# Fourteen of 24 attention units turn their keys by VectorE blocks and transfers through DRAM instead of TensorE transposes

## The chip, the cores and the metric

The kernel runs on one core of one Trainium2 chip. The metric is the device time of one execution in microseconds (us); lower is better. Times are medians of several executions; the profile is of one further execution. In it PE is TensorE's matmuls and PEld its weight loads, DVE is VectorE, ACT ScalarE, POOL GpSimd and SP SyncE, which here only issues transfers (DMAs).

## The reference: what is computed

A gated linear attention over 4 batches, 8 heads, 768 steps and head size 48, whose output goes, as 3072 tokens of 384 features, through a gated two-layer network of width 1536, all in float32:

```python
for t in range(S):
    state = alpha[:, :, t, :, None] * state + np.einsum('bhd,bhe->bhde', k[:, :, t], v[:, :, t])
    y[:, :, t] = np.einsum('bhd,bhde->bhe', q[:, :, t], state)
x = y.transpose(0, 2, 1, 3).reshape(B * S, H * D)
gate = 1.0 / (1.0 + np.exp(-(x @ w_gate)))
out = (gate * (x @ w_val)) @ w_out
```

## The kernel before

**Tiles and stages.** The tokens go in six groups of 512. For each group the attention has four units, one for every two heads, so 24 units, and the network has twelve steps (f = 0 to 11), one for every 128 of the 1536 hidden features, so 72 steps. Features lie on partitions and tokens along the rows of a tile. The first units run before the network starts; from unit 8 on one unit is woven into every third network step, for the group after the one that the network is at.

**A step** (`step`, L692 on; its products in `products`, L237) multiplies x with the gate and value weights into two of three PSUM banks `gv`, nine matmuls each (three feature tiles, times three because x and the weights are split into a high and a low part). ACT takes the sigmoid of the gate (sg, L705), DVE multiplies (L707), ACT rounds the product to its high part hh (L708), DVE takes the rest hl (L709), and PE adds their products with the output weights into three banks `po` (L717), hh with six matmuls and hl with three, a step or more later.

**A late unit** (`late`, from L590 on) works on chunks of 64 tokens, its two heads on partitions 0 to 47 and 64 to 111. SP loads the first decays of each chunk, the decays and the keys into a tile `in` (L594; two of them). DVE scans the decays from the back into G (L407) and from the front into F (L411), with a few small operations between (L409, L410, L413: the chunk factors dec); POOL multiplies the keys by G in place (L415); ACT copies the chunk starts of G away (L417). SP loads the queries into A (L604), the values v (L606) and their second layout vs (L609); DVE multiplies A by F (L612). The keys have to stand once as they are, for the scores, and once with tokens on partitions (kn), for the states: `turn` transposes them on PE, four matmuls with the identity into a `gv` bank (L428), and ACT copies the bank to kn (L432). There is one kn tile after the first units. Then PE makes the scores (L625) and the states' additions (adds, L631), DVE masks the scores (L641) and runs the states (L654), POOL scales them (L661), and a period later PE makes the outputs (L673). `finish` copies them out (L439), moves them through DMAs to their place in x (L446), where ACT and DVE split x into its two parts (L453, L455).

**What sets the order.** `Plan` collects every operation with a cost, a due time and its readers and writers, plays them through by its own costs and writes each engine's instructions in that order; no engine chooses at run time. A unit's due times are set in `begin` by network steps: y is the step at which the unit is visited, x the one of the unit before, three steps earlier. A transfer counts there by its bytes alone, at 390 GB/s and a fixed share. `SHIFTS` moves the due times of numbered operations.

Of the kernel before, what the change touches and what calls it, by code (L numbers as in the profile page):

```python
# [8 lines left out]
F32 = mybir.dt.float32  # L9
# [9 lines left out]
P = 128  # L19
B, H, S, D = 4, 8, 768, 48  # L20
DM, DF = 384, 1536
C = 128
R = 64
E = 64
# [5 lines left out]
T = 512  # L30
# [7 lines left out]
CH, EH = T // C, T // E  # L38
# [8 lines left out]
def after(key, more):  # L47
    return None if key is None else key + more
# [138 lines left out]
RATE = 390e3  # L187
# [7 lines left out]
def vec(n):  # L195
    return 0.07 + n / 960
# [44 lines left out]
def chunked(ctx, tc, rows, vc, vh, vg, weights_in, out, const, ident, flags, weights, within):  # L241
    nc = tc.nc
    sb = ctx.enter_context(tc.tile_pool(name="sb", bufs=1))
    ps = ctx.enter_context(tc.tile_pool(name="ps", bufs=1, space=bass.MemoryType.PSUM))
    plan = Plan()
# [46 lines left out]
    for tag in ("w11", "w8"):  # L292
        nm, t = borrow(tag, WF + 2)
# [6 lines left out]
    r_kn = ring("kn", 1, CH, P, early=[borrow("w6", CH, P) for _ in range(2)])  # L300
# [10 lines left out]
    starts = sb.tile([P, NG * NP, EH], F32, name="starts")  # L311
# [4 lines left out]
    r_hh, r_hl = ring("hh", 2, T, dtype=F32R), ring("hl", 2, T, dtype=F32R)  # L316
    r_at, r_gv, r_po = ring("at", 2, 512, pool=ps), ring("gv", 3, 512, pool=ps), ring("po", NM, 512, pool=ps)
    r_bank = Ring([r_gv.tiles[1], *r_at.tiles, r_gv.tiles[2]])
    ob = [(f"raw{i // 2}", raws[i // 2][1].bitcast(F32)[:, i % 2 * T:(i % 2 + 1) * T]) for i in range(NM)]

    nc.vector.memset(d1g[C], 0.0)
# [78 lines left out]
    def decays(u, size, t, inn, tin):  # L400

        n, nch = T, T // size
        a0, az, kT = tin[:, 0:nch], tin[:, A_Z:A_K], tin[:, A_K:A_Q]
        over = ["later"] if size == E else []
        (gn, G), (fn, F), (g0n, G0), (decn, dec) = r_G.next(), r_F.next(), r_G0.next(), r_dec.next()
        G0, dec = G0[:, 0:nch], dec[:, 0:nch]
        plan.add("vector", scan(n), t["G"], lambda: nc.vector.tensor_tensor_scan(  # L407
            out=G[:, ::-1], data0=az[:, n:0:-1], data1=d1g[size], initial=0.0, op0=ALU.mult, op1=ALU.add), [(inn, "a"), *over], [gn], port=True)
        plan.add("vector", 0.08, t["G"], lambda: nc.vector.tensor_tensor(out=G0, in0=G[:, 0:n:size], in1=tiny[:, 0:nch], op=ALU.max), [gn], [g0n], port=True)  # L409
        plan.add("vector", 0.09, t["G"], lambda: nc.vector.reciprocal(out=d1f[:, 0:n:size], in_=G0), [g0n], ["d1f"])  # L410
        plan.add("vector", scan(n), after(t["G"], 0.01), lambda: nc.vector.tensor_tensor_scan(  # L411
            out=F, data0=az[:, 0:n], data1=d1f, initial=0.0, op0=ALU.mult, op1=ALU.add), ["d1f", (inn, "a")], [fn], port=True)
        plan.add("vector", 0.07, t["dec"], lambda: nc.vector.tensor_tensor(out=dec, in0=a0, in1=G[:, 0:n:size], op=ALU.mult), [gn, (inn, "a")], [decn], port=True)  # L413
        e = "vector" if u in KEYS else "gpsimd"
        plan.add(e, vec(n) if u in KEYS else pool_(n), t["kt"], lambda: getattr(nc, e).tensor_tensor(  # L415
            out=kT, in0=kT, in1=G, op=ALU.mult), [gn, (inn, "r")], [(inn, "k")], port=True)
        plan.add("scalar", 0.14, t["flag"], lambda: nc.scalar.copy(out=starts[:, u, 0:nch], in_=G[:, 0:n:size]), [gn], [("start", u)])  # L417
        return fn, F, decn, dec

    def bound(u, t, fn, F):  # L420
        plan.add("scalar", act(T) + 0.13, t["flag"], lambda: nc.scalar.activation(  # L421
# [2 lines left out]
    def turn(t, inn, kT, pkn, pk):  # L424

        def turned():
            for c in range(CH):
                nc.tensor.transpose(out=pk[:, c * P:(c + 1) * P], in_=kT[:, c * P:(c + 1) * P], identity=ident)  # L428

        plan.add("tensor", (0.109 * CH + 0.03, 0.9), t["X"], turned, [(inn, "k")], [pkn])  # L430
        knn, kn = r_kn.next()
        plan.add("scalar", act(CH * P), t["kn"], lambda: nc.scalar.copy(  # L432
            out=kn.rearrange("p c d -> p (c d)"), in_=pk[:, 0:CH * P]), [pkn], [knn])
        return knn, kn

    def finish(g, p, t, pyn, py):
# [23 lines left out]
    def unit(u, g, p, t):  # L460

        n, nch = T, CH
        inn, tin = r_in.next()
        for lo, hi, marks in ((0, A_K, "a"), (A_K, WIDTH, "rkq")) if u < NP else ((0, WIDTH, "arkq"),):
            plan.add("sync", (0.475, P * (hi - lo) * 4 / RATE), t["load"] if u else -3000.0 + lo, lambda lo=lo, hi=hi: nc.sync.dma_start(
                out=tin[:, lo:hi], in_=rows[g, p, :, lo:hi]), writes=[(inn, m) for m in marks])
        if g:
            vn, v = r_v.next()
            plan.add("sync", (0.475, P * CH * 2 * D * 4 / RATE), after(t["load"], 0.2), lambda: nc.sync.dma_start(
                out=v.rearrange("p c j e -> p (c j e)"), in_=vc[g, p]), writes=[(vn, "v")])  # L470
        else:
            vn, vw = r_vg.next()
            plan.add("sync", (0.475, P * CH * GAP * 4 / RATE), t["load"] if u else -1500.0, lambda: nc.sync.dma_start(
                out=vw.rearrange("p c e -> p (c e)"), in_=vg[p]), writes=[(vn, "v")])
            v = vw.rearrange("p c (o e) -> p c o e", o=1)
            v = [vw[:, :, R * j:R * j + D] for j in range(2)]
        vj = (lambda c, j: v[:, c, j]) if g else (lambda c, j: v[j][:, c])
        kT, qT = tin[:, A_K:A_Q], tin[:, A_Q:WIDTH]
        fn, F, decn, dec = decays(u, C, t, inn, tin)
        e = t["e_q"]  # L480
        plan.add(e, vec(n) if e == "vector" else pool_(n), t["q"], lambda: getattr(nc, e).tensor_tensor(
            out=qT, in0=qT, in1=F, op=ALU.mult), [(inn, "r"), fn], [(inn, "q")], port=True)
# [21 lines left out]
        an, A = r_A.next()  # L504
# [85 lines left out]
    def late(u, g, p, t):  # L590
# [3 lines left out]
        plan.add("sync", (0.475, P * A_Q * 4 / RATE), t["load"], lambda: nc.sync.dma_start(  # L594
            out=tin[:, 0:A_Q], in_=rows[g, p, :, 0:A_Q]), writes=[(inn, m) for m in "ark"])
        kT = tin[:, A_K:A_Q]
        fn, F, decn, dec = decays(u, E, t, inn, tin)
        pkn, pk = r_gv.next()
        knn, kn = turn(t, inn, kT, pkn, pk)
        (an, A), (vn, v), (vsn, vs) = r_A.next(), r_v.next(), r_vs.next()  # L600
        own = [slice(R * j, R * j + R) for j in range(2)]
        other = own[::-1]
# [32 lines left out]
            scores()  # L635
            adds()

        plan.add("tensor", (0.13 * EH + 0.1, 0.5), t["A"], both, [(inn, "k"), (an, 2), (an, 3), knn, (vn, "v")], [x[0] for x in pas])
        for j, (pan, pa) in enumerate(pas):
            for i in range(2):  # L640
                plan.add("vector", 0.43, t["mask"], lambda pa=pa, j=j, i=i: nc.vector.tensor_tensor(  # L641
# [111 lines left out]
    def visit(u):  # L753

        return NF * (u // NP - 1) + 7 - 3 * (NP - 1 - u % NP)

    def begin(u):
        g, p = divmod(u, NP)
        if u < EARLY:
            t = dict.fromkeys(("load", "G", "dec", "kt", "q", "X", "kn", "Y", "A", "mask", "S", "sd", "out", "y"))  # L760
            t.update(flag=14.0 + u, run=1, e_q="vector" if u in QUERIES else "gpsimd")
            return unit(u, g, p, t)
        if u < 2 * NP:
            t = dict.fromkeys(("load", "more", "G", "dec", "kt", "q", "kn", "X", "A", "mask", "S", "sd", "out", "y"))
            return late(u, g, p, {**t, "flag": 14.0 + u})
        y, x = visit(u), visit(u - 1)
        t = dict.fromkeys(("load", "more", "G", "dec", "kt", "q", "kn"))
        if True:
            t = dict(load=x - 2.5, G=x - 0.9, kt=x - 0.7, dec=x, kn=x + 0.6, more=y - 2.0, q=y - 1.0)
        t.update(flag=y + 1 + 0.5 * p, X=after(x, 0.53), A=y + 0.5, mask=y + 0.6, S=y + 0.65, sd=y + 1.2, out=visit(u + 1) + 0.52, y=None)  # L770
        return late(u, g, p, t)

    n_units = NG * NP
# [48 lines left out]
CASTS = ((3, 0), (4, 0), (5, 0), (8, 0), (9, 1))  # L822
QUERIES = (0, 1, 4)
KEYS = (0, 1, 3, 4, 6, 7)
SHIFTS = ((5, -2), (12, -4), (51, 8), (52, 5), (54, 8), (71, 6), (82, 2), (85, 1), (93, -8), (126, 3), (143, 4), (160, 9), (170, 1), (177, 5), (179, 2), (187, 10), (219, -1), (222, 21), (237, -1), (282, 12), (290, -5), (302, 3), (324, 3), (325, -4), (338, 4), (343, -8), (347, -13), (348, -1), (355, 2), (360, 2), (370, 2), (373, 6), (374, 9), (376, 6), (388, 2), (402, 2), (403, 4), (416, -4), (418, 6), (440, -5), (464, -10), (468, 34), (480, -3), (493, 5), (494, 4), (503, -2), (519, 16), (565, -3), (573, -2), (583, 6), (588, -2), (598, -1), (601, 7), (622, -4), (658, 3), (695, 2), (795, 12), (817, 8), (848, 2), (851, -1))
WARM = 29
APART = 24


# [162 lines left out]
```

## Time and profile before

| | |
|---|---|
| median of three runs | 522.94 us (522.88 to 524.06) |
| the profiled execution | 524.13 us, of which the span from its first to its last instruction is 522.4 us |
| PE, PEld, DVE, ACT, POOL busy | 511.0, 434.4, 335.8, 181.9, 95.8 us |
| granted TensorE clock, mean | 0.996 |

The page puts the engine of the last-ending chain beside the busy shares. Busy time is of one engine over the whole span; what a stretch of the program waits for is read from its windows and its timeline. A timeline row merges equal instructions that follow each other: start, length, engine, line, operation, output <- inputs, count, and in brackets the engine's idle time before it and what ended it.

### The profile page before, as it was taken

The page shows a single profiled execution, that of the slowest core. Times are in us where ns is not written, and L with a number is a line of the kernel's source. Part 1 is how long each engine was busy: PE and PEld are TensorE (multiplying, and loading weights), DVE is VectorE, ACT ScalarE, POOL GpSimd, SP SyncE. Part 2 cuts the span into 40 slices and gives each one's busy share as a digit, 9 for nine tenths or more (in the row PEclk, how much of TensorE's full clock was granted, in tenths as well). Part 3 has the DMA queues.
Part 4 walks back from the last instruction along what each step waited for, and adds up shares of the span by engine and source line. Part 5 has one row for each costly group of instructions (what it writes and reads, how often), then busy time and mean ns, then how long its engine had stood idle before and what let it go on. Part 6 is the DMA issues. An engine that isn't in the chain of part 4 may idle for free.

```text
span 522.4 us, 10493 instructions
## 1 busy us (share of the span) xinstructions
PE 511.0 (98%) x4279; PEld 434.4 (83%) x4279; DVE 335.8 (64%) x646; ACT 181.9 (35%) x343; POOL 95.8 (18%) x112
## 2 busy tenths in 40 slices
PE   8999999999999999999999999999999999999994
PEld 4878888788888888888888888888888888888884
DVE  7899999998856884657558648567666342222222
ACT  2447665663323233223233323232323222211221
POOL 4450202213303320302213123032021010000000
PEclk9999999999999999999999999999999999999998
DMA  8747985661321311502303503213312000100001
GB/s 317 285 139 229 310 267 180 186 198 60 107 80 29 107 60 48 168 14 93 107 2 107 163 6 108 81 28 107 120 48 53 1 15 16 61 0 0 2 1 65
DMA packets 22647, 51.83 MB, mean 99 GB/s; under 512 B 3520, under 2 KB 8896, under 8 KB 22592
## 3 DMA queue, kind: packets, MB, share of 16 engines
q1 hardware_dynamic: 22160, 50.22, 30.5%
q0 software_dynamic: 432, 0.88, 1.0%
q8 instruction: 34, 0.56, 0.4%
q14 instruction: 21, 0.17, 0.1%
HBM read 41.55 MB, written 4.72 MB: 89 GB/s over the span
## 4 chain that ended last, share of the span: by engine, by line
PE 85%; DVE 11%; DMA 1%; issue 1%; ACT 0%; DVEq 0%
PE gv L237 49%; PE po L717 26%; PE gv L673 3%; PE at L625 2%; PE gv L428 2%; DMA in<-in_rows_dram 1%; DVE G L407 1%; DVE F L411 1%; DVE w L379 1%; PE at L631 1%; DVE raw L369 1%; DVE first_w L369 1%; DVE hl L709 1%; DVE gv L707 0%; PE at L493 0%
## 5 line engine op out<-in xcount | busy, mean ns | idle before, releaser
L237 PE MATMUL gv<-x,w 128*128 128x512 f32 x1296 | 302.5, 380 | 1.1 <-DVE st L521 0.7
L237 PEld LDWEIGHTS gv<-x,w 128*128 128x128 f32 x1296 | 244.0, 189 | 37.5 <-DVE st L521 1.1
L707 DVE TENSOR_TENSOR gv<-gv,sg 128x512 f32<-128x512 f32 x72 | 50.2, 697 | 140.0 <-PE gv L237 138.5
L717 PE MATMUL po<-hh,w 128*128 128x512 f32 x432 | 109.6, 385 | 0.1
L717 PEld LDWEIGHTS po<-hh,w 128*128 128x128 f32 x432 | 79.7, 189 | 12.3 <-ACT hh L708 0.7
L661 POOL TENSOR_TENSOR vs<-st,dec 64x384 f32<-64x384 f32 x36 | 41.8, 1160 | 260.8 <-DVE st L654 259.5
L708 ACT CAST hh<-gv 128x512 fp32r<-128x512 f32 x72 | 42.1, 585 | 130.1 <-DVE gv L707 124.2
L705 ACT ACTIVATE sg<-gv 128x512 f32<-128x512 f32 x72 | 42.9, 596 | 108.4 <-PE gv L237 106.9
L709 DVE TENSOR_TENSOR hl<-gv,hh 128x512 fp32r<-128x512 f32 x72 | 49.5, 687 | 20.9 <-ACT hh L708 18.8
L717 PE MATMUL po<-hl,w 128*128 128x512 f32 x216 | 60.7, 381 | 0.0
L717 PEld LDWEIGHTS po<-hl,w 128*128 128x128 f32 x216 | 40.7, 189 | 6.5 <-DVE hl L709 0.9
L654 DVE SCALAR_TENSOR_TENSOR st<-st,dec,at 128x48 f32<-128x48 f32 x144 | 38.0, 264 | 4.3
L407 DVE TENSOR_TENSOR_SCAN G<-in,d1g 128x512 f32<-128x512 f32 x22 | 33.8, 1534 | 3.7 <-DMA in<-in_rows_dram 1.8
L641 DVE TENSOR_TENSOR A<-at,mask 64x256 f32<-64x256 f32 x72 | 30.2, 419 | 3.7 <-PE at L631 3.0
L612 DVE TENSOR_TENSOR A<-A,F 64x512 f32<-64x512 f32 x36 | 28.6, 795 | 0.9 <-DMA A<-in_rows_dram 0.3
L415 POOL TENSOR_TENSOR in<-in,G 128x512 f32<-128x512 f32 x17 | 23.0, 1350 | 26.3 <-PE gv L428 17.3
L411 DVE TENSOR_TENSOR_SCAN F<-in,d1f 128x512 f32<-128x512 f32 x22 | 26.8, 1220 | 0.5
L421 ACT ACTIVATE F<-F 128x512 f32<-128x512 f32 x23 | 14.5, 630 | 18.8 <-DVE A L612 16.3
L673 PEld LDWEIGHTS gv<-A,vs 128*48 128x48 f32 x576 | 17.1, 123 | 3.4 <-DVE A L641 2.2
L673 PE MATMUL gv<-A,vs 128*48 128x64 f32 x576 | 19.8, 222 | 0.0
L625 PEld LDWEIGHTS at<-A,in 48*64 48x64 f32 x576 | 10.2, 134 | 6.7 <-issue 5.6
L428 PE MATMUL gv<-ident,in 128*128 128x128 f32 x88 | 14.2, 285 | 0.8 <-DVE in L415 0.6
(136 smaller groups left out, 335.7 us busy)
## 6 DMA issues: line engine op xcount, KB each, us to landing
in<-in_rows_dram SPq DMA_DIRECT2D x18, 516.5 KB, 4.4
raw<-in_w_dram SPq DMA_DIRECT2D x14, 577.0 KB, 4.0
first_w<-in_w_dram SPq DMA_DIRECT2D x8, 577.0 KB, 4.6
A<-in_rows_dram SPq DMA_DIRECT2D x36, 128.0 KB, 3.7
out_dram<-raw SPq DMA_DIRECT2D x18, 256.0 KB, 2.2
v<-in_vc_dram SPq DMA_DIRECT2D x20, 192.0 KB, 4.8
vs<-in_vh_dram SPq DMA_DIRECT2D x36, 96.0 KB, 3.4
x<-yt SPq DMA_DIRECT2D x30, 96.0 KB, 2.8
```

Of the source, the lines that this page charges most:

```text
L237: nc.tensor.matmul(out=dst, lhsT=lhs(a, i), rhs=rhs(b, i), start=(n == 0 and i == 0), stop=(n == len(todo) - 1 and i == NK - 1))
L407: plan.add("vector", scan(n), t["G"], lambda: nc.vector.tensor_tensor_scan(out=G[:, ::-1], data0=az[:, n:0:-1], data1=d1g[size], initial=0 ...
L411: plan.add("vector", scan(n), after(t["G"], 0.01), lambda: nc.vector.tensor_tensor_scan(out=F, data0=az[:, 0:n], data1=d1f, initial=0.0, o ...
L641: plan.add("vector", 0.43, t["mask"], lambda pa=pa, j=j, i=i: nc.vector.tensor_tensor(out=A[other[j], j].rearrange("p (c i t) -> p i c t", ...
L654: nc.vector.scalar_tensor_tensor(out=st[:, c + 1, :], in0=st[:, c, :], scalar=dec[:, c:c + 1], in1=pas[c % 2][1][:, T // 2 + c // 2 * D:T ...
L661: plan.add("gpsimd", pool_(EH * D), t["sd"], lambda j=j: nc.gpsimd.tensor_tensor(out=vs[own[j], j], in0=st[own[j], 0:EH], in1=dec[own[j]]. ...
L673: nc.tensor.matmul(out=py[R * j:R * j + D, cs], lhsT=vs[r, j, c, :], rhs=A[r, j, cs], start=True, stop=True)
L705: plan.add("scalar", act(T), first(0.3), lambda: nc.scalar.activation(out=sg, in_=got["g"][1][:, 0:T], func=AF.Sigmoid), [got["g"][0]], [sgn])
L707: plan.add("vector", vec(T), first(0.4), lambda: nc.vector.tensor_tensor(out=pv, in0=pv, in1=sg, op=ALU.mult), [sgn], [pvn])
L708: plan.add("scalar", act(T), first(0.45), lambda: nc.scalar.copy(out=hh, in_=pv), [pvn], [hhn])
L709: plan.add("vector", vec(T), first(0.5), lambda: nc.vector.tensor_tensor(out=hl, in0=pv, in1=hh, op=ALU.subtract), [pvn, hhn], [hln])
L717: nc.tensor.matmul(out=pso_now[m][1][:, 0:T], lhsT=weights.part("o", b, f)[:, m * P:(m + 1) * P], rhs=halves(h[a]), start=(f == 0 and i == ...
```

## The change

From unit 10 on (`CARRIED = 10`; 14 units) PE's transposes and ACT's copy go. In `carry`, DVE transposes the decayed keys in blocks of 32x32 into G, whose values nobody needs any longer then; SP stores the blocks to a DRAM tile `way` and loads them back into kn in four transfers, one for each 32 partitions, so that each block comes to its place. A block's rows are 32 numbers, so every contiguous piece of these transfers is 128 bytes. ACT's copy of the chunk starts of G gets its own due time, ahead of the transpose. The matmuls of a unit's scores and adds wait for all four loads. The numbers in `SHIFTS` are moved with the added operations; nothing else of the table differs.

```diff
+    dram = ctx.enter_context(tc.tile_pool(name="dram", bufs=1, space=bass.MemoryType.DRAM))
+    r_way = Ring([(f"way{i}", dram.tile([16, P, 32], F32, name=f"way{i}")) for i in range(2)])
...
-        plan.add("scalar", 0.14, t["flag"], lambda: nc.scalar.copy(out=starts[:, u, 0:nch], in_=G[:, 0:n:size]), [gn], [("start", u)])
-        return fn, F, decn, dec
+        plan.add("scalar", 0.14, t.get("first", t["flag"]), lambda: nc.scalar.copy(out=starts[:, u, 0:nch], in_=G[:, 0:n:size]), [gn], [("start", u)])
+        return fn, F, decn, dec, gn, G
...
+    def carry(t, inn, kT, gn, G):
+
+        plan.add("vector", vec(T), t["turn"], lambda: nc.vector.transpose(
+            out=G.rearrange("p (m c j) -> p m c j", m=4, c=CH), in_=kT.rearrange("p (c m i) -> p m c i", c=CH, m=4)), [(inn, "k")], [gn], port=True)
+        wn, way = r_way.next()
+        plan.add("sync", (0.475, P * T * 4 / RATE), t["away"], lambda: nc.sync.dma_start(
+            out=way.rearrange("x (b i) j -> (b i) x j", b=4), in_=G.rearrange("p (x j) -> p x j", j=32)), [gn], [wn])
+        knn, kn = r_kn.next()
+        for m in range(4):
+            plan.add("sync", (0.475, P * C * 4 / RATE), t["back"], lambda m=m: nc.sync.dma_start(
+                out=kn[32 * m:32 * m + 32].rearrange("p c (b j) -> p (c b) j", b=4),
+                in_=way[CH * m:CH * m + CH].rearrange("c (b i) j -> i (c b) j", b=4)), [wn], [(knn, m)])
+        return knn, kn
...
-        fn, F, decn, dec = decays(u, E, t, inn, tin)
-        pkn, pk = r_gv.next()
-        knn, kn = turn(t, inn, kT, pkn, pk)
+        fn, F, decn, dec, gn, G = decays(u, E, t, inn, tin)
+        carried = "turn" in t
+        if carried:
+            knn, kn = carry(t, inn, kT, gn, G)
+        else:
+            pkn, pk = r_gv.next()
+            knn, kn = turn(t, inn, kT, pkn, pk)
...
-        plan.add("tensor", (0.13 * EH + 0.1, 0.5), t["A"], both, [(inn, "k"), (an, 2), (an, 3), knn, (vn, "v")], [x[0] for x in pas])
+        plan.add("tensor", (0.13 * EH + 0.1, 0.5), t["A"], both, [(inn, "k"), (an, 2), (an, 3), knn, *((knn, m) for m in range(4)), (vn, "v")], [x[0] for x in pas])
...
+        if u >= CARRIED:
+            t.update(first=x - 0.6, turn=x - 0.4, away=x - 0.2, back=x + 0.6)
...
+CARRIED = 10
```

**What moves.** On PE at a unit's visit, before: `at` and `gv` are PSUM banks, `kn` the turned keys, `in` the input tile with the decayed keys, `ident` the identity.

```order
L631 MATMUL at_120<-v_80,kn_85 48x48 x2
L428 MATMUL gv_122<-ident,in_79 128x128 x4
L673 MATMUL gv_121<-A_88,vs_90 48x64 x16
L717 MATMUL po_124<-hh_116,w_1050 128x512 x2
L717 MATMUL po_125<-hh_116,w_1050 128x512 x2
L717 MATMUL po_126<-hh_116,w_1050 128x512 x2
L237 MATMUL gv_123<-x_681,w_1287 128x512 x9
```

The same place now (line numbers are 20 higher or so):

```order
L651 MATMUL at_120<-v_80,kn_85 48x48 x2
L693 MATMUL gv_122<-A_88,vs_90 48x64 x16
L737 MATMUL po_124<-hh_116,w_1054 128x512 x2
L737 MATMUL po_125<-hh_116,w_1054 128x512 x2
L737 MATMUL po_126<-hh_116,w_1054 128x512 x2
L237 MATMUL gv_123<-x_685,w_1291 128x512 x9
```

The transposes are gone from between the adds and the outputs; nothing else moved at this place.

On SP, one unit of a group's middle, before: `in` is the input load, `x<-yt` the outputs' way to x.

```order
L594 DMA in_78<-in_rows_dram 128x1033
L606 DMA v_80<-in_vc_dram 128x384
L604 DMA A_88<-in_rows_dram 64x512 x2
L609 DMA vs_90<-in_vh_dram 64x384 x2
L446 DMA x_681<-yt_86 32x512
L446 DMA x_681<-yt_86 16x512
L446 DMA x_681<-yt_86 48x512
```

And now:

```order
L443 DMA way_130<-G_92 128x16x32
L610 DMA in_78<-in_rows_dram 128x1033
L447 DMA kn_85<-way_130 32x16x32 x4
L624 DMA A_88<-in_rows_dram 64x512 x2
L629 DMA vs_90<-in_vh_dram 64x384 x2
L626 DMA v_80<-in_vc_dram 128x384
L462 DMA x_685<-yt_86 32x512
L462 DMA x_685<-yt_86 16x512
L462 DMA x_685<-yt_86 48x512
```

The store stands ahead of the next input load, the four loads of kn between it and A, and v has gone behind vs; x keeps its place at the end.

On PE at the end of a group, before: `x_112` with `w_395` is the first product of the new group, `po` the output banks of the old one.

```order
L717 MATMUL po_124<-hl_117,w_1165 128x512
L237 MATMUL gv_122<-x_112,w_395 128x512 x9
L717 MATMUL po_125<-hl_117,w_1165 128x512
L717 MATMUL po_126<-hl_117,w_1165 128x512
L237 MATMUL gv_123<-x_112,w_395 128x512 x9
L717 MATMUL po_125<-hh_116,w_1287 128x512 x2
```

And now:

```order
L737 MATMUL po_124<-hl_117,w_1169 128x512
L737 MATMUL po_125<-hl_117,w_1169 128x512
L737 MATMUL po_126<-hl_117,w_1169 128x512
L737 MATMUL po_125<-hh_116,w_1291 128x512 x2
L737 MATMUL po_124<-hh_116,w_1291 128x512 x2
L737 MATMUL po_126<-hh_116,w_1291 128x512 x2
L237 MATMUL gv_122<-x_112,w_399 128x512 x9
L237 MATMUL gv_123<-x_112,w_399 128x512 x9
```

The new group's first products have gone behind two hl and six hh matmuls of the old one; so at two of the group ends. DVE's transpose stands in most units right behind dec (L413, now L415), or behind the subtraction of x (L455, now L471) where one stands there, and ahead of the next gate product.

## Rows read from the trace of the kernel before

**Rows 1.** The page: busy us by engine, one queue, the last-ending chain.

```profile
PE 511.0 (98%) x4279; PEld 434.4 (83%) x4279; DVE 335.8 (64%) x646; ACT 181.9 (35%) x343; POOL 95.8 (18%) x112
...
q1 hardware_dynamic: 22160, 50.22, 30.5%
...
PE 85%; DVE 11%; DMA 1%; issue 1%; ACT 0%; DVEq 0%
```

**Rows 2.** Windows: stretch, length, busy PE, PEld, DVE, ACT, POOL, clock, DMA share, GB/s.

```profile
320.00:360.00 40.00, 40.00 (x361) 34.59 (x361) 25.59 (x53) 12.45 (x24) 8.24 (x8) 1.00 0.24 70
```

**Rows 3.** Timeline of PE over one period: start us, length us.

```profile
313.44 0.69 PE L625 MATMUL at<-A,in 48*64 48x64 f32 x32
...
314.43 0.66 PE L428 MATMUL gv<-ident,in 128*128 128x128 f32 x4
315.01 1.10 PE L673 MATMUL gv<-A,vs 128*48 128x64 f32 x32
...
329.10 2.11 PE L237 MATMUL gv<-x,w 128*128 128x512 f32 x9
...
333.72 0.70 PE L625 MATMUL at<-A,in 48*64 48x64 f32 x32
```

**Rows 4.** Line 428 from 120 to 400 us: count, ns min/median/max, first, last start.

```profile
L428 PE MATMUL gv<-ident,in x56: 272/273/332, 131.8 to 395.9; 128*128 128x128 f32 x56
```

**Rows 5.** Groups by form on DVE: count, busy us, mean ns, idle before.

```profile
L407 DVE TENSOR_TENSOR_SCAN G<-in,d1g 128x512 f32<-128x512 f32 x22 | 33.8, 1534 | 3.7 <-DMA in<-in_rows_dram 1.8 <-POOL vs L661 1.7 <-issue 0.2
...
L737 DVE COPY raw<-po 128x512 f32<-128x512 f32 x5 | 3.4, 681 | 0.0
```

**Rows 6.** Timeline of POOL, the keys times G.

```profile
321.70 1.28 POOL L415 TENSOR_TENSOR in<-in,G 128x512 f32<-128x512 f32 x1
```

**Rows 7.** Timeline of DVE in the same period.

```profile
322.86 1.39 DVE L612 TENSOR_TENSOR A<-A,F 64x512 f32<-64x512 f32 x2
324.28 0.69 DVE L709 TENSOR_TENSOR hl<-gv,hh 128x512 fp32r<-128x512 f32 x1
...
326.46 0.15 DVE L413 TENSOR_TENSOR dec<-in,G 128x8 f32<-128x8 f32 x1
326.53 0.69 DVE L455 TENSOR_TENSOR x<-x 128x512 fp32r<-128x512 f32 x1
328.07 0.70 DVE L707 TENSOR_TENSOR gv<-gv,sg 128x512 f32<-128x512 f32 x1 [0.86 <-PE gv L237]
```

**Rows 8.** DMA from 289.5 to 293.9: rate in 40 slices, queue (packets, MB, share), issue to landing.

```profile
GB/s 0 0 0 0 0 0 0 0 0 0 242 428 354 335 465 354 354 335 447 372 354 428 391 335 372 428 354 372 354 75 0 0 0 0 0 149 0 0 0 0
...
q1 hardware_dynamic: 432, 0.79, 47.9%
...
out_dram<-raw SPq DMA_DIRECT2D x3, 256.0 KB, 2.3
```

**Rows 9.** DMA from 313 to 326, a unit's transfers: queue and one load.

```profile
q1 hardware_dynamic: 752, 1.38, 36.1%
...
in<-in_rows_dram SPq DMA_DIRECT2D x1, 516.5 KB, 3.4
```

**Rows 10.** Waits of SP's queue: total us, times, longest.

```profile
SPq L594 <- PE at L625: 128.4, 14, 14.7
```

**Rows 11.** Timeline of SP, the input load.

```profile
314.23 0.33 SPq L594 DMA_DIRECT2D in<-in_rows_dram  x1
```

**Rows 12.** Timeline of PE and DVE at the end of a group.

```profile
362.54 1.46 PE L717 MATMUL po<-hh,w 128*128 128x512 f32 x6
362.81 0.70 DVE L707 TENSOR_TENSOR gv<-gv,sg 128x512 f32<-128x512 f32 x1 [1.24 <-PE gv L237]
363.42 0.68 DVE L455 TENSOR_TENSOR x<-x 128x512 fp32r<-128x512 f32 x1
...
363.84 0.38 PE L717 MATMUL po<-hl,w 128*128 128x512 f32 x1
...
364.05 2.11 PE L237 MATMUL gv<-x,w 128*128 128x512 f32 x9
```

More of the change, by code (lines that the diff above doesn't have):

```diff
@@ L478, in unit @@
         kT, qT = tin[:, A_K:A_Q], tin[:, A_Q:WIDTH]
-        fn, F, decn, dec = decays(u, C, t, inn, tin)
+        fn, F, decn, dec, gn, G = decays(u, C, t, inn, tin)
         e = t["e_q"]
@@ L824 @@
 KEYS = (0, 1, 3, 4, 6, 7)
-SHIFTS = ((5, -2), (12, -4), (51, 8), (52, 5), (54, 8), (71, 6), (82, 2), (85, 1), (93, -8), (126, 3), (143, 4), (160, 9), (170, 1), (177, 5), (179, 2), (187, 10), (219, -1), (222, 21), (237, -1), (282, 12), (290, -5), (302, 3), (324, 3), (325, -4), (338, 4), (343, -8), (347, -13), (348, -1), (355, 2), (360, 2), (370, 2), (373, 6), (374, 9), (376, 6), (388, 2), (402, 2), (403, 4), (416, -4), (418, 6), (440, -5), (464, -10), (468, 34), (480, -3), (493, 5), (494, 4), (503, -2), (519, 16), (565, -3), (573, -2), (583, 6), (588, -2), (598, -1), (601, 7), (622, -4), (658, 3), (695, 2), (795, 12), (817, 8), (848, 2), (851, -1))
+SHIFTS = ((5, -2), (12, -4), (51, 8), (52, 5), (54, 8), (71, 6), (82, 2), (85, 1), (93, -8), (126, 3), (143, 4), (160, 9), (170, 1), (177, 5), (179, 2), (187, 10), (219, -1), (222, 21), (237, -1), (282, 12), (290, -5), (302, 3), (324, 3), (325, -4), (338, 4), (343, -8), (347, -13), (348, -1), (355, 2), (360, 2), (370, 2), (373, 6), (374, 9), (376, 6), (388, 2), (402, 2), (403, 4), (416, -4), (418, 6), (440, -5), (464, -10), (468, 34), (480, -3), (493, 5), (494, 4), (503, -2), (519, 16), (565, -3), (573, -2), (583, 6), (588, -2), (598, -1), (601, 7), (622, -4), (658, 3), (699, 2), (803, 12), (829, 8), (860, 2), (863, -1))
 WARM = 29
+CARRIED = 10
 APART = 24
```

## The prediction, before the change was run

> **What bounds the kernel now.** I read the busy shares first: TensorE (PE) is busy 511.0 of 522.4 us, VectorE (DVE) 335.8, ScalarE 181.9, GpSimd 95.8, and the chain that ended last is 85% PE [rows 1]. A busy PE may still hide waits, so I read the stage that the change touches by its windows: from 320 to 360 us PE is busy 40.00 of 40.00 us at full granted clock, while the DMA engines are used to 0.24 and DVE 25.6 of 40 us [rows 2]. So in this stretch a microsecond taken from PE's list is a microsecond of the run, unless something else comes late. The timeline of PE then gives the period: the score matmuls of two successive units start at 313.44 and 333.72, 20.28 us apart [rows 3]. The change asks two questions: what do the transposes occupy on PE, and does the new way of kn, through 4096 small pieces a unit, fit into 20 us.
>
> **What goes.** The four transposes of a unit start at 314.43 and the output matmuls behind them at 315.01: 0.58 us of PE's list, not the 0.66 us of modelled busy time [rows 3]. From 120 us on there are 56 of them, so 14 units of four [rows 4]: 14 x 0.58 = 8.1 us. The output matmuls need the masks and states of the unit before, a period old, so they can move up at once. ScalarE's copy of kn also goes; ScalarE waits most of its time, so it counts nothing.
>
> **What DVE gets.** One transpose of 128x512 per unit, which the trace does not show. The nearest rows of that shape are a copy at 681 ns and, as upper end, a scan at 1534 ns [rows 5]; I take 0.69 us. It needs the decayed keys, which GpSimd has at 322.98 [rows 6], and stands behind dec, at 326.6, or behind the x subtraction, at 327.2. The next DVE instruction waits for PE until 328.07 [rows 7], so 0.69 us fits, and 1.53 us would delay the gate product by 0.7 us. The PE step that eats such a product comes microseconds later: hl, ended by 324.97, holds a bank that PE takes at 329.10 [rows 3, 7]. That is 4.1 us of slack, and hides either end. The starts copy, now due before the turn writes over G, is a 0.2 us item of an engine with room, and G's next writer comes a period later, when the store has long read it.
>
> **The waits that come in.** The turn waits for the keys, and behind it stands the gate product; the store waits for the turn, and behind it the next input load, which waits for PE in any case; the kn loads wait for the store's landing and for the adds that free kn, and behind them stand A, vs, v and the x transfers; the adds wait for kn, and behind them the outputs. As built, a transfer also waits for the landing of the eighth before it; with 14 a unit in place of 9 the x transfers so wait for kn, which is ahead of them in the queue anyway.
>
> **What the queue gets.** Per unit one store of 2048 pieces of 128 B and four loads of 512 such pieces, 128 pieces for each of the 16 DMA engines both ways. Call their data times w and k. No row shows pieces of this size. A dense store of three times 128 rows of 2 KB kept the engines busy for 47.9% of 4.4 us, 33.7 us summed over 16, for 432 packets; its best slice ran at 465 GB/s, 29 bytes per ns and engine, so 0.79 MB are 27.2 us and 6.5 us are left, 15 ns per packet [rows 8]. A 128 B piece is then 15 + 4 = 19 ns, and w = 128 x 19 ns = 2.5 us. The same sum for a unit's loads (36.1% of 13 us x 16 = 75.1 us, 47.6 of them bytes, 752 packets) leaves 37 ns per packet, 41 ns for a piece and 5.3 us [rows 9]. The lower end is bytes alone, 0.6 us; the upper end is that a piece costs what a 2 KB packet does, 33.7 / 384 = 88 ns, 11.2 us. The new transfers are long and dense like the store, the loads' engines were often between transfers, so I take w = 2.5 and k = 3.2, with 5.3 as k's likely top.
>
> Does it fit? The wait for the store's landing costs nothing while it ends before SP turns to the loads. The store is issued when the turn ends, about 328.0 - 20.3 = 307.7 for the loads at 314.7; it lands after 1.6 us (2.3 less 0.7 of data [rows 8]) plus w, 311.8. SP had been idle there: it waits 128.4 us in 14 times for the input buffer that the scores free [rows 10]. The kn loads then stand right behind the input load (issue 314.23, landing 3.4 us later, 317.6 [rows 9, 11]) and in front of A and vs, which wait behind them. A lands at 317.6 + k + 0.7 for its own bytes: 321.5 at k = 3.2, 323.6 at 5.3. Its first reader is DVE's A multiply at 322.86, 322.3 in the shorter period [rows 7]. So A is in time, or 1.3 us late, inside the 4.1 us. kn itself is needed a period later.
>
> There is a loop in it, and it gives the limit: A lands, A multiply to dec 3.75 us, x 0.69, turn 0.69; store 1.6 + w; loads 2.1 (3.4 less 1.3 of data) + k; A's bytes 0.7; A lands. That is 9.5 + w + k against a period of 20.28 - 0.58 = 19.7 us, so w + k may be 10.2 us, 40 ns a piece. My values make 5.7, the likely top 7.8.
>
> The page "DMA: Bandwidth & Descriptors" of the Trainium skill, section "Why small descriptors are slow (HBM only)", puts some three cycles on each packet beside its 32-byte beats, by its clock an estimated 8 ns for 128 B; by that w and k would be 1 us each and only the 0.5 us at the group ends below would remain. The store row, 15 ns beyond the bytes, stands above it.
>
> **Where something is late.** At a group's end x is just in time now: its subtraction on DVE starts at 363.42 and takes 0.68, PE's first gate matmul of the new group starts at 364.05 [rows 12]. In the new order PE does two hl and six hh matmuls first at two of the ends, 0.42 + 1.30 us by the starts of one hl and six hh now, so it wants x at 364.05 + 1.72 - 0.58 = 365.2. DVE has then the gate product until 362.9, two A multiplies (1.39), hl (0.69), x (0.69): 365.7, or, where A lands at 323.6 + 40.6 = 364.2, 367.0. So 0.5 to 1.8 us are lost, at the three group ends with kn loads in front of x; I take 0.7 each, 2.1 us.
>
> **Sum.** -8.1 + 2.1 = -6.0 us on the profiled execution's own 524.13 us (span 522.4 and 1.7 around it), 518.1; the median of the three runs is 522.94, 1.2 us below that execution, and gives 516.9 us. About 0.3%, 1.6 us, is what a measurement of this kernel can tell from no change.
>
> **Rivals.**
> *Small pieces are dear, the loop binds (slower).* If a piece costs more than 40 ns both ways, each unit's A lands later than the last one's, by 9.5 + w + k - 19.7 us a round, first into the 4.1 us of slack and then onto PE. At 55 ns, halfway between 20 and 88, w + k = 14.1 and a round loses 3.9 us: 13 rounds are 51, less 4, so 516.9 + 47 = 564 us. At 88 ns it is 12.3 us a round, 156 in all, 673 us. For it: the transfers so far have rows of 1.5 KB and more, and the pieces, 14 x 4096 = 57,344, outnumber the queue's 22,160 packets of the whole run before [rows 1]. Against it: the dense store's 15 ns. Chance 0.28.
> The same page's section "Specifications" says that below 512 B the DMA does a read-modify-write; if a piece then costs two passes of a 512 B one, an estimate is 2 x 33 ns for the store and some 55 ns for the load, w + k = 15.5 and a run near 580 us. No row of the run before shows data in pieces below 512 B.
> *The gain is given back at the group ends and to late A's (about no change).* With pieces near 40 ns the loop just closes, A is 1 to 4 us late in most units, and the three ends lose 1.8 us or more each, with another 1 to 2 us where the first carried units start out of step: -8.1 + 5.4 + 1.5 = -1.2, 521.7 us. For it: the x row has no slack at all [rows 12]. Against it: it needs a narrow band of piece costs. Chance 0.20, half of it beyond 1.6 us below the median.
> *As forecast*, 514.8 (nothing late anywhere: 522.94 - 8.1) to 519: 0.52.
>
> **Numbers.** Faster: 0.52 + 0.10 = 0.62; same: 0.10; slower: 0.28. The range goes from 514 (the full 8.1 us and the spread of the runs) into the slow case up to 545, some 50 ns a piece, leaving out the dearer pieces, about 0.17, and little below. The likeliest case alone is 514.8 to 519.
>
> **What the profile after would show.** PE without the four transposes, the outputs 0.58 us sooner behind the scores; a DVE transpose near 0.7 us; a period of 19.7 us between score matmuls from 130 to 400 us. w from the store's issue to landing, about 4.1 us, k from the landing of A behind the kn loads. If the loop binds, DVE's A multiply waits on the DMA of A in every unit, PE's idle grows, and its wait names hl or the gate product. If only the ends lose, PE idles before the new group's first gate matmul, released by the x subtraction. I am wrong if the period stays at 20.28 with PE full, since then the transposes filled a hole, or if the store takes over 8 us.

## The result, and the profile after

The changed kernel takes 515.08 us (median of 6 runs, 514.85 to 515.44) against 523.18 us (median of 6, 522.88 to 524.06): ratio 0.9844, 95% interval 0.9831 to 0.9856. Forecast were 516.9 us and "faster". The profiled execution took 515.34 us, its span 513.6.

The page of the changed kernel shows the busy us by engine, the queue and the chain that answer to [rows 1]:

```profile
PE 503.1 (98%) x4223; PEld 428.3 (83%) x4223; DVE 346.9 (68%) x660; ACT 172.3 (34%) x329; POOL 95.8 (19%) x112
...
q1 hardware_dynamic: 80624, 57.56, 41.4%
...
PE 86%; DVE 10%; DMA 1%; issue 1%; ACT 0%; POOL 0%; DVEq 0%; ACTq 0%; POOLq 0%
```

PE has 56 matmuls and 7.9 busy us less, DVE 11.1 us more, the queue 58,464 packets more; the share of PE in the last-ending chain is nearly as before. The window that answers to [rows 2] (columns as there) is still full, with the DMA engines used 0.42 in place of 0.24:

```profile
320.00:360.00 40.00, 40.00 (x358) 34.67 (x357) 28.60 (x56) 10.78 (x22) 8.26 (x7) 1.00 0.42 97
```

So the gain must be a shorter list, not fewer waits. PE's timeline answers to [rows 3]: scores, adds and outputs of one unit, the scores of the next, and the scores at either end of the stretch in which the 14 units lie.

```profile
130.25 0.69 PE L645 MATMUL at<-A,in 48*64 48x64 f32 x32
...
307.73 0.69 PE L645 MATMUL at<-A,in 48*64 48x64 f32 x32
308.25 0.54 PE L651 MATMUL at<-v,kn 64*48 64x48 f32 x32
308.72 1.10 PE L693 MATMUL gv<-A,vs 128*48 128x64 f32 x32
...
327.43 0.69 PE L645 MATMUL at<-A,in 48*64 48x64 f32 x32
...
406.24 0.69 PE L645 MATMUL at<-A,in 48*64 48x64 f32 x32
```

The outputs start with the end of the adds; from scores to scores it is 19.70 us, as forecast, where it was 20.28 [rows 3]. The whole stretch, 130.25 to 406.24, takes 275.99 us. The kernel before has its scores at these places:

```profile
130.85 0.69 PE L625 MATMUL at<-A,in 48*64 48x64 f32 x32
...
414.86 0.70 PE L625 MATMUL at<-A,in 48*64 48x64 f32 x32
```

That is 284.01 us, so 8.02 us went, 0.573 a unit. From scores to scores 13 of the 14 units save 0.59 us. One saves 0.43: near 190 us the transposes stood behind a gate product, the outputs stand there now, and behind it their weight loads pause 0.33 us of their own (PE's weight loads of the changed kernel):

```profile
190.51 0.95 PEld L693 LDWEIGHTS gv<-A,vs 128*48 128x48 f32 x32 [0.33 <-POOL vs L681]
```

The spans differ by 8.8; of the rest 0.6 lies ahead of the stretch and 0.2 behind it. Ahead of it the program is nearly the same, but the start of the stretch differs between traces by up to 2.1 us. So below the stretch is compared beside the time.

The rest of the forecast's terms. DVE's groups by form, for [rows 5] (columns as there), show the new transpose:

```profile
L440 DVE STREAM_TRANSPOSE G<-in 128x512 f32<-128x512 f32 x14 | 9.9, 708 | 0.8
```

The DMA view from 301 to 308 us holds one store and no other transfer of the kernel, and answers to [rows 8] (rate in 40 slices, packets, MB and share of 16 engines, issue to landing):

```profile
GB/s 0 94 0 0 0 0 0 0 0 0 0 48 165 148 143 146 148 146 143 143 148 115 6 0 0 0 0 0 0 0 0 0 0 0 0 0 0 0 0 0
...
q1 hardware_dynamic: 2064, 0.26, 24.6%
...
way<-G SPq DMA_DIRECT2D x1, 256.0 KB, 3.2
```

24.6% of 7 us x 16 engines are 27.6 us of engine time, 13.4 ns a packet; a store's 128 pieces per engine take w = 1.7 us, at some 146 GB/s. From 151.5 to 154.0 only pieces run, mostly loads back:

```profile
q1 hardware_dynamic: 1813, 0.23, 59.4%
```

59.4% of 2.5 us x 16 are 23.8 us, 13.1 ns a packet, so k's data are 1.7 us as well. But SP's timeline, in the period of the scores at 307.73 (start and length in SP's queue), shows that data are not what the loads cost:

```profile
302.05 0.39 SPq L443 DMA_DIRECT2D way<-G  x1
308.52 0.34 SPq L610 DMA_DIRECT2D in<-in_rows_dram  x1
309.00 2.38 SPq L447 DMA_DIRECT2D kn<-way  x4
311.48 1.99 SPq L624 DMA_DIRECT2D A<-in_rows_dram  x2
```

The four issues take 2.38 us (1.9 to 3.3 in other periods), and A stands behind them. The store has landed at 302.05 + 3.2 = 305.3, more than 3 us before the loads' turn. In the waits of SP's queue (total, times, longest), for [rows 10], the wait for PE ahead of the load of in has shrunk from 128.4 us, and the wait for the turn stands in the same idle time:

```profile
SPq L443 <- DVE G L440: 73.6, 13, 16.0
SPq L610 <- PE at L645: 52.6, 13, 6.0
```

The Trainium skill's page "DMA: Bandwidth & Descriptors", section "Why small descriptors are slow (HBM only)", gave the prediction an estimate of 8 ns a piece; measured are 13, about as far above that as below the 19 ns that the sum took from the dense store of long rows. The two-pass cost that the prediction estimated from its "Specifications" (55 to 66 ns a piece) does not show here.

### The profile page after: what moved, and what is told of

The parts are those of the page before. It is cut to its first block, busy times and chain, and to the rows that moved or that the text cites. A ratio compares the mean times of both kernels' runs of the same rounds, so it can differ in the third digit from the quotient of the medians.

```text
span 513.6 us, 10505 instructions
## 1 busy us (share of the span) xinstructions
PE 503.1 (98%) x4223; PEld 428.3 (83%) x4223; DVE 346.9 (68%) x660; ACT 172.3 (34%) x329; POOL 95.8 (19%) x112
## 4 chain that ended last, share of the span: by engine, by line
PE 86%; DVE 10%; DMA 1%; issue 1%; ACT 0%; POOL 0%; DVEq 0%; ACTq 0%; POOLq 0%
PE gv L237 49%; PE po L737 26%; PE gv L693 3%; PE at L645 2%; PE gv L704 1%; DVE w L381 1%; PE at L651 1%; DVE raw L371 1%; DMA in<-in_rows_dram 1%; DVE G L409 1%; DVE first_w L371 1%; DVE F L413 1%; PE at L509 1%; DVE hl L729 1%; DVE A L661 1%
## 5 line engine op out<-in xcount | busy, mean ns | idle before, releaser
L632 DVE TENSOR_TENSOR A<-A,F 64x512 f32<-64x512 f32 x36 | 32.1, 893 | 2.2 <-DMA A<-in_rows_dram 1.7
L413 DVE TENSOR_TENSOR_SCAN F<-in,d1f 128x512 f32<-128x512 f32 x22 | 27.7, 1258 | 0.5
L419 ACT COPY starts<-G 128x8 f32<-128x8 f32 (+1 forms) x23 | 4.7, 203 | 33.1 <-DVE G L409 33.1
```

## The experiments

The theory: the gain is PE's list, 0.57 us for each unit, and turn, store and loads are hidden. The rivals: it comes from the new order or from something else the change frees; the transfers sit close to a limit. Each ratio is to the kernel before, run beside it; "stretch" is the time between the two score bursts as above.

Apart from e9, which edits the kernel before, the runs edit the changed kernel. Each of these also numbers the operations without the added ones, so that `SHIFTS` still moves the same operations; the code below leaves that out, and `...` marks other cuts.

| run | us, median | ratio, 95% interval | stretch, us |
|---|---|---|---|
| the change | 515.08 | 0.9844, 0.9831 to 0.9856 | 275.99 |
| e1, 7 units | 519.25 | 0.9932, 0.9919 to 0.9945 | 279.94 |
| e2, 16 units | 520.86 | 0.9958, 0.9945 to 0.9971 | 275.98 |
| e3, unread transposes too | 520.59 | 0.9957, 0.9944 to 0.9970 | 281.50 |
| e4, nobody turns | 516.01 | 0.9858, 0.9843 to 0.9874 | 275.93 |
| e5, loads twice | 517.74 | 0.9887, 0.9871 to 0.9904 | 278.55 |
| e6, loads four times | 587.45 | 1.1237, 1.1177 to 1.1297 | 345.8 |
| e7, low part first | 516.50 | 0.9863, 0.9846 to 0.9879 | 277.27 |
| e8, turn three times | 516.73 | 0.9870, 0.9853 to 0.9886 | 277.71 |
| e9, before, swapped | 521.06 | 0.9961, 0.9949 to 0.9973 | 281.74 |
| e10, unread, ahead | 523.14 | 1.0001, 0.9992 to 1.0010 | 284.01 |
| e11, 15 units | 515.56 | 0.9852, 0.9837 to 0.9867 | 275.98 |
| e12, extra loads early | 516.67 | 0.9874, 0.9856 to 0.9891 | 276.65 |

### Does each unit bring its share?

```diff
-CARRIED = 10
+CARRIED = 17
```

> Only the last 7 of the 14 units (the eighteenth on) go by way of DRAM; the first 7 of them are turned by TensorE as before. Theory (the gain is TensorE's list made shorter, one unit at a time, and everything else is hidden): 7 x 0.575 = 4.0 us of gain, so about 519.1 us, half-way between 523.2 and 515.1. Rival 1 (the gain comes from the new written order or from fewer users of the gv banks, not from each unit): not half-way; either most of the gain is there already (516 or less) or hardly any (522 or more). Rival 2 (the transfers cost something that each carried unit pays): more than half of the gain would be left over, below 519.

519.25 us, and a stretch shorter by 4.07 us: 7 x 0.58. The gain goes unit by unit.

### Is anything of the new way on the path?

```diff
-            knn, kn = carry(t, inn, kT, gn, G)
+            knn, kn = r_kn.next()
```

> Nobody turns the keys of the 14 units: VectorE's block transposes, the stores and the loads are left out, and the additions to the states read whatever lies in the tile. Theory (turn, store and loads are hidden): 515.1 us, within 0.4 us. Rival 2 (pieces, issue times or VectorE's 0.7 us are partly on the path): below 514.5; every 0.04 us per unit that they cost shows as 0.5 us.

The stretch is 275.93 us, the changed kernel's to 0.06 us; the median, 0.9 us higher and so outside the 0.4 expected, owes nothing to it (here the stretch begins 0.8 us later). 14 turns, stores and 56 loads cost PE nothing in the changed kernel.

### Is it the transposes themselves?

```diff
             knn, kn = carry(t, inn, kT, gn, G)
+            pkn, pk = r_gv.next()
+            def also():
+                for c in range(CH):
+                    nc.tensor.transpose(out=pk[:, c * P:(c + 1) * P], in_=kT[:, c * P:(c + 1) * P], identity=ident)
+            plan.add("tensor", (0.109 * CH + 0.03, 0.9), t["X"], also, [(inn, "k")], [pkn], extra=True)
```

> As the changed kernel, but TensorE also makes the four transposes of each carried unit into a gv bank, whose values nobody reads; ScalarE's copy stays away. Theory (TensorE's list): the whole gain is taken back, about 523.2 us (522.5 to 523.8). Rival 1 (the gain comes from the order, or from ScalarE's 14 copies of 0.6 us that are gone, or from a key tile that is ready earlier): a good part of the gain stays, 515 to 520 us.

Neither: 520.59 us, 2.6 below before and above the rival's 515 to 520. The stretch takes back 5.51 us, 0.39 a unit, and 2.51 us stay. PE's timeline of this run shows what is different:

```profile
311.67 0.54 PE L661 MATMUL at<-v,kn 64*48 64x48 f32 x32
312.14 1.10 PE L703 MATMUL gv<-A,vs 128*48 128x64 f32 x32
313.17 0.66 PE L624 MATMUL gv<-ident,in 128*128 128x128 f32 x4
313.58 1.54 PE L747 MATMUL po<-hh,w 128*128 128x512 f32 x6
```

The written order came out with the transposes behind the outputs, and there they take 0.41 us from start to start. In the kernel before they stand ahead of the outputs and take 0.58. Its weight loads (PEld, idle time and its inferred end in brackets) say where the 0.17 us lie:

```profile
314.43 0.42 PEld L428 LDWEIGHTS gv<-ident,in 128*128 128x128 f32 x4
315.01 0.95 PEld L673 LDWEIGHTS gv<-A,vs 128*48 128x48 f32 x32 [0.17 <-DVE A L641]
```

The trace names the mask multiply, L641, which ends at that time, in 13 of the 14 units. The theory for the next two runs is that it is not the cause, and that a gap belongs between transposes and outputs. The first has no transfers at all; it is the kernel before with the outputs due a little earlier, which swaps the two in 13 units:

```diff
-sd=y + 1.2, out=visit(u + 1) + 0.52, y=None)
+sd=y + 1.2, out=visit(u + 1) + (0.52 if u < 9 else 0.5), y=None)
```

> The kernel before with all its transposes, but from the eleventh late unit on TensorE does the previous unit's outputs ahead of this unit's four transposes instead of behind them (13 places). Theory (of the 0.58 us that the four transposes took from start to start, 0.41 are their own and 0.17 a gap that stands only between them and outputs that follow): 13 x 0.17 = 2.2 us of gain without any transfer, about 521.0 us, and the gap of 0.17 us ahead of the outputs' first weight load is gone. Rival (the gap belongs to the outputs and moves with them, or the gain left over with the unread transposes came from ScalarE's copies): 523.2, no change.

521.06 us, the stretch 2.27 us shorter, 0.175 for each of the 13 on the average: twelve gain some 0.19, and the unit near 190 us gains nothing, since there too the outputs now stand behind a gate product. In the twelve the outputs' weight loads begin ahead of the mask multiply (which starts at 312.34 here) and without a gap:

```profile
312.23 0.95 PEld L673 LDWEIGHTS gv<-A,vs 128*48 128x48 f32 x32
```

The second is e3 with the unread transposes due earlier, so that they stand ahead of the outputs again:

```diff
-t["X"], also, [(inn, "k")], [pkn], extra=True)
+t["X"] - 0.2, also, [(inn, "k")], [pkn], extra=True)
```

> As the changed kernel with the unread transposes, but these stand ahead of the previous unit's outputs, where the kernel before had them. Theory (as above): the gap is back, 14 x 0.58 us of TensorE's list are restored and the whole gain is gone: 523.0 us, within 0.7. Rival (what was left over, 2.6 us, came from the transfers' side: no copy on ScalarE, a key tile that is ready earlier): 520.6 as with the transposes behind.

523.14 us and a stretch of 284.01, the kernel before's to the hundredth, with all the turns and transfers running beside it. In its weight loads the gap is back, 0.16 to 0.17 us in each of the 14 units. The trace names the mask multiply again in 12 of them, but not in this one:

```profile
313.39 0.42 PEld L624 LDWEIGHTS gv<-ident,in 128*128 128x128 f32 x4
313.98 0.95 PEld L703 LDWEIGHTS gv<-A,vs 128*48 128x48 f32 x32 [0.17 <-issue]
```

Here the mask multiply still runs, until 314.09, when the outputs' weight loads begin at 313.98, and the gap is the same, so they do not wait for it (timeline of DVE):

```profile
313.67 0.42 DVE L671 TENSOR_TENSOR A<-at,mask 64x256 f32<-64x256 f32 x1
```

So a unit's 0.58 us are 0.41 of transposes and 0.17 of a gap behind them, and nothing comes from ScalarE, the banks or the key tile. Why PE stops between transposes and outputs, and not between transposes and the products of L747, no run shows.

### How near is the limit?

```diff
+    spare = [dram.tile([P, CH, P], F32, name=f"spare{i}") for i in range(1)]
...
-            plan.add("sync", ..., t["back"], lambda m=m: nc.sync.dma_start(
-                out=kn[32 * m:32 * m + 32]...
+            plan.add("sync", ..., t["back"], lambda m=m: [nc.sync.dma_start(
+                out=to[32 * m:32 * m + 32]...
+                in_=way[...]) for to in (kn, *spare)], [wn], ...
```

> As the changed kernel, but each of the four loads of turned keys is issued twice, the second time into a scratch in DRAM that nobody reads: 8 issues of about 0.48 us and 56 x 64 KB more in 128-byte pieces. Theory (the round of turn, store, four loads, scores' operand A, its multiply takes some 16.5 us of the 19.7 us that TensorE needs, so about 3.3 us are free; the four more issues take 1.9 us of them): 515.1 us, within 0.5. Rival (the transfers already set the pace or share the path): 14 x 1.9 = 27 us more, about 542, or a part of it.

517.74 us, 2.6 us on the stretch: the miss is small beside the rival's 27 us, but real. The period stays at 19.7 us in most units; the loss lies mainly in two places. In the one near 183 us, in the middle of a group, SP issues so (the queue's starts and lengths):

```profile
176.48 0.53 SPq L451 DMA_DIRECT2D spare<-way  x1
177.11 1.21 SPq L628 DMA_DIRECT2D A<-in_rows_dram  x2
```

A is issued 4.2 us later than in the changed kernel's trace (172.93 there, though its stretch began 0.5 us later), and DVE's multiply waits for it:

```profile
180.11 1.40 DVE L636 TENSOR_TENSOR A<-A,F 64x512 f32<-64x512 f32 x2 [2.81 <-DMA A<-in_rows_dram]
```

And ScalarE takes its list in order: the pass over F waits for A's multiply, and behind it stand the rounding of x to its high part and the sigmoid of a gate product.

```profile
181.55 0.63 ACT L427 ACTIVATE F<-F 128x512 f32<-128x512 f32 x1 [4.01 <-DVE A L636]
...
182.40 0.62 ACT L473 CAST x<-x 128x512 fp32r<-128x512 f32 x1
182.92 0.59 ACT L729 ACTIVATE sg<-gv 128x512 f32<-128x512 f32 x1
```

For that sigmoid, which frees a bank, PE waits (the trace's inference, as in all these brackets):

```profile
183.57 2.21 PE L240 MATMUL gv<-x,w 128*128 128x512 f32 x9 [0.95 <-ACT sg L729]
```

At the other place, near 281 us at the start of a new group, the rounding of x itself waits for the moves of y, and PE for it. With four copies of each load:

```diff
-    spare = [dram.tile([P, CH, P], F32, name=f"spare{i}") for i in range(1)]
+    spare = [dram.tile([P, CH, P], F32, name=f"spare{i}") for i in range(3)]
```

> Each of the four loads is issued four times, three times into scratch: 16 issues, 5.7 us more of SyncE's queue per unit. Theory: 3.3 us of it are free and the rest, about 2.4 us a unit, is paid: 515 + 14 x 2.4 = 549 us, between 535 and 560, and TensorE waits at the scores for VectorE's multiply of A. Rival (transfers never matter here, TensorE's list alone does): 515.

587.45 us: the loop closes, and harder than expected. From SP's timeline of a unit, first and last of the 16 issues and A's behind them:

```profile
277.58 0.36 SPq L451 DMA_DIRECT2D kn<-way  x1
...
286.75 1.86 SPq L451 DMA_DIRECT2D spare<-way  x3
288.71 1.21 SPq L628 DMA_DIRECT2D A<-in_rows_dram  x2
```

From the first issue to A's it is 11.1 us, 0.70 an issue, not 0.48; the changed kernel's four take 1.9 to 3.3. In these 11.1 us the DMA engines were busy 0.70, so their data alone did not fill it. With some 8 us more against 3.3 us free (the store of the changed kernel landed 3.2 us ahead of the next issue, 305.3 to 308.52), 4.7 x 14 = 66 us, and 515 + 66 = 581, near the measured time. That is an estimate, and part of its closeness may be luck: PE's granted clock also fell, to 0.90 to 0.97 in windows from 190 to 430 us, and no run separates what that cost. DVE's groups show where it arrives, the multiply of A, before it idle 96.9 us in place of 2.2:

```profile
L636 DVE TENSOR_TENSOR A<-A,F 64x512 f32<-64x512 f32 x36 | 24.7, 685 | 96.9 <-DMA A<-in_rows_dram 96.3
```

PE's waits from 130 to 430 us (total, times, longest) name hl above all, and x at three group ends. At the scores, where the expectation put the wait, stands one of 5.4 us, for which the trace names nobody:

```profile
PE gv L240 <- DVE hl L733: 20.2, 8, 3.3
PE gv L240 <- ACT x L473: 13.7, 3, 5.8
```

Is it the packets or the place in the queue? The doubled loads again, as parts of their own, which the planner puts behind the store, ahead of the next load of in; the other engines' order is the changed kernel's:

```diff
+    spare = [dram.tile([P, CH, P], F32, name=f"spare{i}") for i in range(1)]
...
+        for again in range(1):
+            for m in range(4):
+                plan.add("sync", ..., t["back"], lambda m=m, again=again: nc.sync.dma_start(
+                    out=spare[again][32 * m:32 * m + 32]..., in_=way[CH * m:CH * m + CH]...), [wn], ...
```

> The same four extra loads as in the kernel with 8 loads a unit, but SyncE issues them right behind the store, ahead of the next unit's load of in, where its queue was waiting for TensorE (52.6 us in 13 units of the changed kernel); the order on the other engines is the changed kernel's. Theory (those 2.4 us came from the place in SyncE's queue: A's and x's transfers were issued about 2.4 us later, and at two group ends x's split came late; pieces and packets as such are free): 515.4 us, ratio 0.985, within 0.7. Rival (twice the packets cost something wherever they are issued): 517 to 518 as before.

Between the two. (The expectation's "two group ends" is wrong in one: near 183 us it was the sigmoid that came late.) The stretch loses 0.66 us where e5 lost 2.56, so most of e5's loss is the place in the queue. The median, 516.67, stands 1.6 us above the changed kernel's, of which the stretch explains 0.7; its interval touches the changed kernel's. In one unit, near 190 us, the extra issues stand between the loads of kn and A all the same, and A is issued at 194.28, 2.6 us later than in the changed kernel.

VectorE's time by itself, the block transpose three times:

```diff
-        plan.add("vector", vec(T), t["turn"], lambda: nc.vector.transpose(
-            out=G.rearrange(...), in_=kT.rearrange(...)), [(inn, "k")], [gn], port=True)
+        plan.add("vector", vec(T), t["turn"], lambda: [nc.vector.transpose(
+            out=G.rearrange(...), in_=kT.rearrange(...)) for again in range(3)], [(inn, "k")], [gn], port=True)
```

> As the changed kernel, but VectorE makes its block transpose three times, which is 2 x 0.71 = 1.42 us more on VectorE per unit and as much later for the store. Theory (VectorE's list and the round have over 3 us free): 515.1 us, within 0.6. Rival (VectorE's time is on the path): up to 14 x 1.42 = 20 us more, 535.

516.73 us, 1.6 above the changed kernel where 0.6 was allowed. Of the 20 us that DVE got, 1.72 reach the stretch, all in one period, most of it around a group's first products (timeline of PE; a wait of 0.34 us for an hl stands earlier, at 185.98):

```profile
199.62 0.59 PE L240 MATMUL gv<-x,w 128*128 128x512 f32 x2
200.99 3.80 PE L240 MATMUL gv<-x,w 128*128 128x512 f32 x16 [0.78 <-ACT x L472]
```

DVE's own lateness is hidden; A's multiply, at 195.73 in the changed kernel and 198.31 here, holds up ScalarE, and that the rounding of x.

### Why did the group ends lose nothing?

The prediction let PE want the subtraction of x, its low part, when the group's first product starts. PE, its weight loads and DVE at such an end in the changed kernel, which answers to [rows 12] (one fence each, since they are three answers of the timeline):

```profile
358.31 3.00 PE L237 MATMUL gv<-x,w 128*128 128x512 f32 x13
```

```profile
358.09 1.05 PEld L237 LDWEIGHTS gv<-x,w 128*128 128x128 f32 x5
359.31 1.81 PEld L237 LDWEIGHTS gv<-x,w 128*128 128x128 f32 x9 [0.16 <-DVE x L471]
```

```profile
358.57 0.68 DVE L471 TENSOR_TENSOR x<-x 128x512 fp32r<-128x512 f32 x1
```

PE starts 0.26 us before the subtraction does, does five of the nine products (three of high with high, two with low tiles that are long there), and only the sixth waits, 0.16 us. So the subtraction ends at 359.25, 0.94 us after PE's start, about as late as the prediction had it. At the end near 281 us it is the same; the period of each is 19.73 us in place of 19.69. At the third, near 200 us, x is done (at 199.17) before PE starts (at 199.42). The experiment puts the low part first in a group's first step:

```diff
-def products(nc, dst, lhs, rhs, tiles=range(NK)):
+def products(nc, dst, lhs, rhs, tiles=range(NK), pairs=PAIRS):
...
+                    ((0, 1), (0, 0), (1, 0)) if g and f == 0 else PAIRS),
```

> As the changed kernel, but in the first step of each later group the three products with the low part of x come first instead of second (the sum is the same, the order of adding differs). Theory (the loss of 0.7 us that was predicted for each group end did not come because the low part is first read at the fourth to sixth product of nine, about 1 us after the step begins): with the low part first, TensorE waits 0.5 to 1.2 us at each of three to five group ends, so 517 to 519.5 us. Rival (VectorE's subtraction was early anyway, and the order of the products hides nothing): no change, 515.1.

516.50 us, the stretch 1.28 us longer, in equal parts at two ends. PE's weight loads waited (total, times, longest):

```profile
PEld gv L240 <- DVE x L474: 1.6, 2, 0.8
```

The theory's place and size per end are shown; but it is two ends, not three to five, so the time stays below the 517 expected, and the interval overlaps the changed kernel's. The order of the products is worth 0.6 us at each.

### Would more units pay?

```diff
-CARRIED = 10
+CARRIED = 8
```

> Sixteen units by way of DRAM instead of 14 (the ninth and tenth too, in the stretch of about 90 to 130 us where TensorE is busy 97 to 100%). Theory: another 2 x 0.575 = 1.15 us, so 513.9 us. Rival (in that stretch VectorE, busy 90 to 96%, sets the pace, and 0.7 us more on it per unit costs as much as TensorE saves): 515 to 516.5 us, no gain or a loss.

520.86 us, worse than the rival's number. The stretch is the changed kernel's; 5.6 us are lost ahead of it, where VectorE is nearly full and weights are loaded too. These are PE's waits from 84 to 140 us, and the window in which the granted clock fell (columns as in [rows 2]; the changed kernel has 1.00 there). The clock is not the main part: the two executions with a mean of 0.997 still took 520.5 and 519.8 us.

```profile
PE po L740 <- ACT hh L731: 1.8, 1, 1.8
PE at L648 <- DVE A L635: 1.8, 2, 0.9
PE at L654 <- DMA kn<-way: 1.1, 2, 0.7
```

```profile
80.00:110.00 30.00, 27.14 (x284) 22.34 (x283) 27.70 (x55) 14.06 (x25) 7.81 (x8) 0.94 0.76 208
```

Here PE waits for the loads themselves. One unit more instead of two:

```diff
-CARRIED = 10
+CARRIED = 9
```

> Fifteen units by way of DRAM, one more than the change (from the tenth). Theory (a unit is worth 0.58 us as long as its round has slack; with the ninth and tenth together TensorE waited for the loads, for the multiply of A and for hh between 90 and 120 us): if the tenth alone still fits, 514.5 us; if the waits come with it too, 517 to 520. The second is the likelier, 0.6, since VectorE is busy 18 of 20 us between 110 and 130 us.

515.56 us, 0.9852 against 0.9844, intervals almost the same: no gain, no loss, between the two outcomes expected; the one called likelier did not come. No version tried beats the change.

## Why the prediction was right, point by point

- **PE full, so its list counts**: right, shown by e1 and e10. The period of 19.7 us came, and 14 x 0.58 = 8.1 came out as 8.02 (0.59 in 13 units, 0.43 in one).
- **0.58 us from start to start, not the modelled 0.66**: right as a price, and for a reason that the prediction did not have. 0.41 are the transposes and 0.17 the gap behind them; whoever had summed the transposes alone (14 x 0.41 = 5.7) would have been 2.3 us short.
- **DVE's 0.69 us, hidden**: 0.71, hidden (e4); three times as much costs 1.7 us in all (e8).
- **w = 2.5, k = 3.2**: 1.7 and 1.7 us of data. The 19 ns added a fixed 15 from long rows to the bytes; 13 is the whole. Too high, but hidden, so the sum does not feel it. What the term k lacked is the issue: 1.9 to 3.3 us in SP's queue for four loads.
- **Loop 9.5 + w + k against 19.7**: the loop exists (e6), and binds, as SP's timeline reads, more through issue times than through data. The store lands more than 3 us before the loads' turn.
- **Group ends, 0.7 each at three, 2.1 in all**: the term that was mis-sized; it measured under 0.1. The subtraction was as late as forecast; the step failed where it put the low part's due time at the first product. It is the sixth, about 1.1 us later, and at the third end x was early. That covers the 1.8 us by which 516.9 missed 515.08. The place was right: x at a group's end is what PE waits for most in e7, e8 and e12, and at one of the two places in e5.
- **Rival of dear pieces (0.28)**: excluded by 13 ns a piece. Its mechanism is what e6 shows, at 11 us in the queue. **Rival of the gain given back (0.20)**: did not come; e5 is a mild form of it.

## What to carry to other kernels

Where PE is full in a stage, price what you take off its list by the starts of the neighbours, gaps included, and try first whether another order saves a part: here the swap of two neighbours alone gave 2.0 of the 8 us (2.3 on the stretch). A round trip through DRAM in 128-byte pieces can be hidden if its round, from load to load, has some us free; count the queue's issues in it, not only the bytes. What a late step hurts first is not always its reader: look at what stands behind it on an in-order engine, as x's rounding and the sigmoid behind the pass that waits for A.

## What was not expected of the hardware

- 128-byte pieces cost 13.4 ns (store) and 13.1 ns (mostly loads) of a DMA engine each.
- One issue of a 512-piece load held SP's queue for 0.5 to 0.8 us, on the average of four in a row; 16 of them 11.1 us.
- Between four fp32 transposes and outputs with weights of 128x48 PE's weight loads paused 0.16 to 0.17 us in every unit of the kernel before and of e10; between the same transposes and 128x512 products (e3, e9) the trace shows no pause. The inferred releaser, an instruction that ended at that moment, was not the cause.
